# Six sums of four tokens on GpSimd instead of VectorE, and a new order of the instruction stream, in a fused attention and MoE kernel

## The chip, the cores and the metric

The kernel runs on one core of one Trainium2 chip. The metric is the device time of one launch in microseconds (us), as the median of several runs. The kernel before takes 362.11 us (three runs, 361.36 to 363.36).

The core has five instruction streams that run side by side [...]: TensorE (PE in the profile; PEld is its weight load), VectorE (DVE), ScalarE (ACT), GpSimd (POOL) and SyncE (SP, used here for DMA issues alone). Each executes its own stream in order.

## The reference, cut to what matters

```python
# q, k, v: (8, 8, 576, 64): batch, heads, tokens, head dimension; all float32
def _attn_ref(q, k, v):
    factor, scale = 4, 1.0 / np.sqrt(64)
    q_d, k_d, v_d = (x.reshape(B, H, S // 4, 4, D).mean(axis=3) for x in (q, k, v))
    out_d = softmax_attention(q_d, k_d, v_d)            # 144 x 144 scores
    out_up = np.repeat(out_d, 4, axis=2)
    mask = np.abs(pos[:, None] - pos[None, :]) < 4      # a band around the diagonal
    out_local = softmax_attention(q, k, v, where=mask)  # 576 x 576 scores, banded
    return out_up + out_local

def _moe_ref(x, w_in, w_out):                           # x: (4608, 512): tokens, heads * head dim
    h = x @ w_in                                        # d_ff = 2048
    g = np.where(h > 0, h, np.exp(np.minimum(h, 0)) - 1)
    return g @ w_out
```

So each token of each head attends to the seven tokens around it, and each group of four tokens attends, through its mean, to all groups. The two outputs are added, and the result goes through two dense products with an ELU between them.

## The kernel before

The kernel is written as a list of short words. One string, `ORDER`, holds all of them, and the kernel calls the function behind each word in turn. A word appends its instructions to the streams of its engines, so the order of the words is the order of the instructions on each engine; no scheduler changes it later.

```python
NINES, PE_SPREAD, HP4 = (0, 1, 2), (0, 1, 2), 12
X_DVE, K_DVE = ((0, 3, 0),), ((0, 0), (0, 1))
F_POOL = ()
ORDER = """
KM Lq0.0 KS KE Lk0.0 FILL TBL Lq0.1 KV Lk0.1 Lq0.2 KN Lk0.2 KI Cq0.0 KX Ck0.0 Lq0.3 Tq0.0 Lk0.3
... [cut]
"""
...
    ctx.enter_context(tc.manual_schedule())
    banks_as(("t", 4, 512))                       # batch 0: four single PSUM banks
    for word in ORDER.split():
        if word == "Q0":
            banks_as(("misc", 2, 512), ("hp", 2, 512))
        ...
        does[name](*numbers_of_the_word)
```

The numbers of a word are batch and pair of heads (there are eight batches of four pairs), or tile numbers of the MoE part. The words that matter here:

- `Lq Lk Lv`: load q, k or v of a pair through SyncE's queue. `Dq Dk b.h`: load two pairs of q or k through GpSimd's queue, converting to fp16. `WI WO`: load a quarter of w_in or w_out through GpSimd's queue.
- `Cq Ck Cv`: cast a loaded tile to fp16, on GpSimd.
- `Tq Tk`: transpose q or k with TensorE into PSUM. `Aq Ak`: copy them to SBUF (ScalarE; the k of pairs 0.0 and 0.1 by VectorE).
- `Fq Fk`: sums of four neighbouring tokens of the transposed q or k, for batches 0, 1 and 2 (`NINES`). Later batches get these sums out of TensorE together with the transposition.
- `SC` (batch 0: `SL` and `SD`): local scores, then scores of the groups. The latter read what `F` wrote.
- `E0 E1` (batch 0: `G H`): exponentials, ScalarE. `M`: the band mask, VectorE.
- `VS VD`: sums of four of v, TensorE, and their copy, VectorE. `OUT`: both attention outputs, TensorE. `DEN RC`: softmax denominators and their reciprocals. `RB`: reciprocals spread over partitions by TensorE. `LG MUL X`: outputs to SBUF, scaled, and added into the MoE input tile `xt`.
- `mm1.t.c` and `Q`: first MoE product, token tile t, d_ff tile c, four matmuls of 512 columns. `e m g`: exponential on ScalarE, then two VectorE instructions that make the ELU. `mm2.t.i`: a quarter of the second product of a 128-token tile. `oc st`: eviction by ScalarE and store.
- `Z1` to `Z3`: one to three filler matmuls, which compute nothing that is used. They go into the PSUM tile that the next word opens.
- `WL`: a one-element GpSimd write to a buffer; the next v load into that buffer waits for it. This word holds loads of v back.

The parts that the change touches or that its steps lead through:

```python
def load_half(n, b, h):                           # Dq, Dk
    t = sb.tile([128, 2, LR * D], FP16, tag=n + "2", bufs=2, name=n + "2")
    nc.gpsimd.dma_start(out=t[:], in_=...)        # fp32 in HBM, fp16 in SBUF

def hold(*_):                                     # WL
    t = stage("held")
    nc.gpsimd.memset(t[0:1, 0:1], 0.0)
    held.append(t)

def cast_v(b, j):                                 # Cv
    t = sb.tile([KW, NB, 2, D], FP16, tag="v16", bufs=7, name="v16")
    nc.gpsimd.tensor_copy(out=t[:], in_=...)

def fours(n, b, j):                               # Fq, Fk
    if n == "q":
        qt = stT[(b, j)][0]
        to, x = qt[:, S:RW], qt[:, 0:S]
    else:
        kt, kd = stT[(b, j)][-2:]
        to, x = kd[:], kt[:, PAD : PAD + S]
    x = x.rearrange("p (n h) -> p n h", h=4)      # 128 partitions, 144 groups of 4
    if (n, b, j) in F_POOL:
        f = sb.tile([128, SD], FP32, tag="four", bufs=1, name="four")
        nc.gpsimd.tensor_tensor(out=f[:], in0=x[:, :, 0], in1=x[:, :, 1], op=AB.add)
        nc.gpsimd.tensor_tensor(out=f[:], in0=f[:], in1=x[:, :, 2], op=AB.add)
        nc.gpsimd.tensor_tensor(out=to, in0=f[:], in1=x[:, :, 3], op=AB.add)
        return
    nc.vector.tensor_reduce(out=to, in_=x, axis=mybir.AxisListType.X, op=AB.add)

def elu_min(t, fc):                               # m
    nc.vector.tensor_scalar(out=e[:], in0=e[:], scalar1=1.0, scalar2=-1.0,
                            op0=AB.min, op1=AB.add)

def elu_add(t, fc):                               # g: reads the PSUM tile hp, and so frees it
    nc.vector.scalar_tensor_tensor(out=gts[t][:, fc, :], in0=hps[(t, fc)][:], scalar=0.0,
                                   op0=AB.max, in1=els.pop((t, fc))[:], op1=AB.add)
```

Of the kernel before, what the change touches and what calls it, by code (L numbers as in the profile page):

```python
# [51 lines left out]
g.0.1 Ak1.0 WLv2.0 Dq2.0 e.0.4 Fq1.1 Tk1.1 e.0.3 X0.2.1 mm1.0.7 Fk1.0 X0.3.1 Dk2.0 Ak1.1 m.0.3
g.0.3 SC1.0 m.0.4 mm1.0.9 E01.0 Fk1.1 m.0.2 E11.0 g.0.2 g.0.4 SC1.1 e.0.7 Cv1.0 Lv1.3 mm1.0.10
e.0.9 m.0.7 E01.1 g.0.7 mm1.0.6 M1.0 e.0.10 mm1.0.5 E11.1 m.0.9 m.0.10 VS1.0 g.0.9 e.0.6 Tq1.3
VD1.0 e.0.5 mm1.0.11 m.0.6 g.0.6 Dq2.1 Aq1.3 OUT1.0 m.0.5 M1.1 Tq1.2 LG1.0 g.0.10 Aq1.2 Tk1.3
Fq1.3 mm1.0.12 e.0.11 Dk2.1 Fq1.2 Ak1.3 Tk1.2 m.0.11 e.0.12 mm1.0.8 Fk1.3 Ak1.2 m.0.12 g.0.12
SC1.3 Cv1.1 Lv2.0 Fk1.2 E01.3 mm1.0.13 g.0.11 E11.3 VS1.1 g.0.5 VD1.1 e.0.8 mm2.0.0 M1.3 e.0.13
m.0.8 SC1.2 g.0.8 mm2.0.1 E01.2 m.0.13 g.0.13 mm1.0.15 E11.2 OUT1.1 e.0.15 M1.2 mm1.0.14 LG1.1
m.0.15 g.0.15 Z2 DEN1 e.0.14 m.0.14 g.0.14 Z1 mm2.0.2 RC1 Cv1.2 Lv2.1 Z1 RB1.0 Z2 VS1.2 MUL1.0
mm2.0.3 VD1.2 X1.0.1 RB1.1 oc.0.0 X1.0.2 OUT1.2 MUL1.1 st.0.0 mm2.0.4 LG1.2 X1.1.2 RB1.2 X1.1.1  # L60
Tq2.0 MUL1.2 mm2.0.5 Aq2.0 X1.2.1 Fq2.0 Tq2.1 Tk2.1 Aq2.1 mm2.0.6 X1.2.2 Ak2.1 Fq2.1 mm2.0.7
Fk2.1 Tq2.3 oc.0.1 Tk2.0 Aq2.3 mm2.0.8 Cv1.3 Lv2.2 st.0.1 Ak2.0 Fq2.3 mm2.0.9 Fk2.0 VS1.3 Tk2.3
VD1.3 Cv2.0 Lv2.3 mm2.0.10 Ak2.3 Fk2.3 OUT1.3 RB1.3 LG1.3 mm2.0.11 Cv2.1 Lq3.0 MUL1.3 VS2.0
oc.0.2 mm2.0.12 VD2.0 X1.3.1 st.0.2 SC2.0 Lk3.0 X1.3.2 mm2.0.13 E02.0 Cv2.2 mm1.1.0 E12.0
mm1.1.6 e.1.0 M2.0 Lv3.0 SC2.3 m.1.0 e.1.6 g.1.0 Cv2.3 mm2.0.14 E02.3 m.1.6 g.1.6 mm1.1.5 E12.3
Cq3.0 Lq3.1 Tq2.2 e.1.5 M2.3 mm1.1.3 Aq2.2 m.1.5 g.1.5 VS2.3 e.1.3 Ck3.0 Lk3.1 OUT2.0 Fq2.2
mm1.1.1 LG2.0 VD2.3 m.1.3 g.1.3 Tk2.2 e.1.1 VS2.1 Cv3.0 Lv3.1 Ak2.2 mm1.1.2 VD2.1 m.1.1 g.1.1
SC2.1 e.1.2 Cq3.1 Lq3.2 mm2.0.15 Fk2.2 E02.1 m.1.2 mm1.1.8 g.1.2 E12.1 Ck3.1 Lk3.2 mm1.1.4
oc.0.3 e.1.8 M2.1 st.0.3 SC2.2 e.1.4 m.1.8 mm2.1.0 g.1.8 E02.2 Cv3.1 Lv3.2 mm1.1.15 E12.2 m.1.4
g.1.4 OUT2.1 e.1.15 Lq3.3 M2.2 mm1.1.7 LG2.1 m.1.15 g.1.15 DEN2 e.1.7 Lk3.3 m.1.7 mm1.1.9 g.1.7  # L70
RC2 VS2.2 e.1.9 mm1.1.10 VD2.2 m.1.9 g.1.9 Cv3.2 Lv3.3 OUT2.2 e.1.10 RB2.2 LG2.2 m.1.10 mm1.1.14
g.1.10 Lq4.0 MUL2.2 OUT2.3 e.1.14 mm1.1.11 LG2.3 m.1.14 g.1.14 X2.2.2 RB2.3 Lk4.0 e.1.11 RB2.1
X2.2.3 MUL2.3 mm1.1.13 MUL2.1 X2.3.2 Tq3.1 e.1.13 Lv4.0 mm2.1.1 m.1.11 Aq3.1 g.1.11 X2.1.2 RB2.0
VD3.1 Cv3.3 mm1.1.12 Lq4.1 MUL2.0 X2.3.3 Tk3.1 e.1.12 m.1.13 mm2.1.2 g.1.13 X2.0.3 Ak3.1 X2.0.2
Tq3.0 KD3.1 m.1.12 Tk3.0 Aq3.0 g.1.12 Cq3.3 mm1.2.0 Ak3.0 VD3.0 Ck3.2 mm1.2.4 e.2.0 KD3.0 Ck3.3
Tq3.3 e.2.4 m.2.0 mm2.1.3 Aq3.3 g.2.0 Cq3.2 Tk3.3 m.2.4 oc.1.0 Lk4.1 mm1.2.11 g.2.4 X2.1.3 Ak3.3
Lv4.1 Cq4.1 VD3.3 mm2.1.4 st.1.0 e.2.11 KD3.3 Cv4.0 Lq4.2 SC3.3 m.2.11 mm1.2.7 g.2.11 E03.3
mm1.2.2 E13.3 mm2.1.5 e.2.7 M3.3 Lk4.2 e.2.2 SC3.1 m.2.7 g.2.7 mm2.1.6 E03.1 m.2.2 g.2.2 Cv4.1
Lv4.2 mm1.2.10 E13.1 Tq3.2 e.2.10 M3.1 Tk3.2 Aq3.2 m.2.10 mm1.2.3 g.2.10 Ck4.1 Lq4.3 Ak3.2 VD3.2
mm2.1.7 Ck4.0 e.2.3 KD3.2 SC3.2 m.2.3 oc.1.1 g.2.3 Cq4.0 mm2.1.8 E03.2 st.1.1 Lk4.3 mm1.2.13  # L80
E13.2 Cv4.2 Lv4.3 mm1.2.14 e.2.13 M3.2 SC3.0 e.2.14 m.2.13 mm2.1.9 E03.0 Lq5.0 g.2.13 m.2.14
mm2.1.10 E13.0 g.2.14 Tq4.1 M3.0 Tk4.1 Lk5.0 Aq4.1 Cq4.3 mm1.2.8 Ak4.1 Ck4.2 VD4.1 DEN3 e.2.8
KD4.1 m.2.8 Lv5.0 Tq4.0 g.2.8 Tk4.0 RC3 Aq4.0 Cq4.2 mm1.2.6 Ak4.0 Lq5.1 Ck4.3 VD4.0 mm1.2.5
e.2.6 KD4.0 SO3 SC4.1 m.2.6 e.2.5 g.2.6 mm2.1.11 Lk5.1 E04.1 m.2.5 g.2.5 mm1.2.15 E14.1 mm1.2.12
oc.1.2 M4.1 Lv5.1 e.2.15 st.1.2 SC4.0 e.2.12 m.2.15 mm2.1.12 g.2.15 E04.0 Lq5.2 m.2.12 mm1.2.9
E14.0 g.2.12 mm1.2.1 SI3 M4.0 Lk5.2 Tq4.2 e.2.9 Tk4.2 mm2.1.13 e.2.1 Ck5.1 Aq4.2 Lv5.2 mm2.1.14
m.2.1 Ak4.2 g.2.1 mm2.1.15 VD4.2 KD4.2 m.2.9 mm2.2.0 oc.1.3 g.2.9 st.1.3 mm2.2.1 SC4.2 mm2.2.2
E04.2 mm2.2.3 E14.2 OUT3.2 oc.2.0 M4.2 OUT3.3 st.2.0 MUL3.2 mm2.2.4 MUL3.3 mm2.2.5 X3.2.4 X3.2.3
OUT3.1 X3.3.4 OUT3.0 MUL3.1 mm2.2.6 X3.3.3 MUL3.0 Cv4.3 mm2.2.7 X3.1.3 Lq5.3 mm2.2.8 oc.2.1
X3.0.4 st.2.1 mm2.2.9 X3.0.3 X3.1.4 Tq4.3 Cv5.0 Tk4.3 Aq4.3 mm1.3.0 Cq5.1 Ak4.3 VD4.3 mm1.3.5  # L90
Cq5.0 e.3.0 KD4.3 SC4.3 m.3.0 e.3.5 Lk5.3 g.3.0 Ck5.0 mm2.2.10 E04.3 m.3.5 Lv5.3 mm1.3.9 g.3.5
Cv5.1 E14.3 Lq6.0 Cv5.2 Tq5.0 e.3.9 mm1.3.1 M4.3 Aq5.0 m.3.9 Tk5.0 e.3.1 VD5.0 DEN4 g.3.9 Ak5.0
Lk6.0 m.3.1 Tq5.1 g.3.1 mm1.3.13 KD5.0 Aq5.1 Cq5.3 RC4 Lv6.0 mm1.3.6 Cq5.2 VD5.1 SO4 e.3.13
Tk5.1 e.3.6 m.3.13 Tq5.2 g.3.13 Ck5.3 Ak5.1 Lq6.1 mm2.2.11 Aq5.2 m.3.6 KD5.1 Ck5.2 mm1.3.2 g.3.6
oc.2.2 VD5.2 Lk6.1 Tk5.2 e.3.2 mm1.3.10 st.2.2 Ak5.2 m.3.2 g.3.2 mm2.2.12 SI4 KD5.2 Lv6.1
mm1.3.4 e.3.10 SC5.0 e.3.4 m.3.10 mm2.2.13 g.3.10 Lq6.2 E05.0 m.3.4 mm1.3.11 E15.0 g.3.4 mm1.3.3
e.3.11 M5.0 SC5.2 m.3.11 e.3.3 g.3.11 Lk6.2 mm2.2.14 E05.2 m.3.3 g.3.3 mm1.3.14 E15.2 mm1.3.8
e.3.14 M5.2 mm2.2.15 m.3.14 e.3.8 g.3.14 OUT4.0 m.3.8 oc.2.3 g.3.8 OUT4.1 Cv5.3 Lv6.2 mm1.3.7
MUL4.0 st.2.3 Cv6.0 mm1.3.15 MUL4.1 e.3.7 X4.0.4 Lq6.3 OUT4.3 m.3.7 e.3.15 g.3.7 X4.1.5 OUT4.2
# [739 lines left out]
```

## Time and profile before

The profile is of one execution. Its span is 361.6 us, and the granted TensorE clock is 0.999.

| | |
|---|---|
| median time | 362.11 us |
| span of the profiled execution | 361.6 us |
| `F` on VectorE (TENSOR_REDUCE, 128 x 576 in, 128 x 144 out) | 24 of 744 to 745 ns |
| `m` (TENSOR_SCALAR) and `g` (SCALAR_TENSOR_TENSOR) | 144 each, mean 350 and 691 ns |
| `mm1` matmuls, `mm2` matmuls | 576 each, mean 379 and 380 ns |
| GpSimd cast of v | 30, mean 847 ns |
| load of v, issue to landing | 28 of 336 KB, median 7.0 us |
| data moved | 45.78 MB, mean 127 GB/s |

How to read it. [...] 379 ns isn't the pace at which 512-column matmuls follow each other: eight in a row take 1.73 us in the chain of waits late in the kernel, 0.216 us each. A group's idle time is that of its engine just ahead of it, with what ended it behind an arrow; an engine that isn't the bound may idle at no cost. A DMA share over 1.00 in a stretch means that packets of several queues were under way on an engine at once.

### The profile page before, as it was taken

The numbers are of one execution on the slowest core, as the hardware profiler recorded it, in microseconds if no ns is written. First come the engines' busy times: TensorE is split into PE (matmuls) and PEld (weight loads), VectorE is DVE, ScalarE is ACT, GpSimd is POOL, SyncE is SP. The second block draws the span as 40 slices with busy tenths as digits, with TensorE's granted clock in tenths as the row PEclk, the third lists the DMA queues.
The fourth block names the chain that finished last, engine by engine and source line by source line (L and its number), as shares of the span: only waits on it lengthen the run. The fifth ranks groups of instructions, "written<-read, shape, count | busy, mean of one in ns | idle before, by whom it ended". The sixth has DMA issues, their size and how long they took to land.

```text
span 361.6 us, 9574 instructions
## 1 busy us (share of the span) xinstructions
PE 350.0 (97%) x3964; PEld 183.4 (51%) x3964; DVE 240.1 (66%) x475; ACT 209.6 (58%) x395; POOL 121.2 (34%) x177
## 2 busy tenths in 40 slices
PE   7999899999999999999999999999999999999995
PEld 3664445554565545565555545554544544444442
DVE  3877996568887774587986675867665845465520
ACT  3855883578568875277587754685554334344421
POOL 6597314372293310860592109401500410000000
PEclk9999999999999999999999999999999999999999
DMA  7989999999968899498909992531004010010012
GB/s 265 176 140 198 197 197 203 201 177 166 189 120 168 152 200 198 128 188 168 205 4 198 170 156 83 83 84 62 29 32 113 30 60 29 29 61 29 30 60 87
DMA packets 106870, 45.78 MB, mean 127 GB/s; under 512 B 92330, under 2 KB 101194, under 8 KB 106826
## 3 DMA queue, kind: packets, MB, share of 16 engines
q1 hardware_dynamic: 96586, 34.61, 49.4%
q0 software_dynamic: 6528, 6.63, 10.9%
q10 hardware_dynamic: 3712, 3.93, 5.5%
q8 instruction: 31, 0.51, 0.6%
q14 instruction: 13, 0.11, 0.1%
HBM read 42.18 MB, written 9.53 MB: 143 GB/s over the span
## 4 chain that ended last, share of the span: by engine, by line
PE 73%; DMA 15%; DVE 5%; POOL 2%; ACT 2%; SPq 1%; issue 1%; ACTq 0%; POOLq 0%; DVEq 0%
PE op L754 31%; PE hp L710 27%; DMA v<-in_v_dram 11%; DMA rcb<-rd 3%; PE sc L528 2%; DVE e L739 2%; PE lg L653 2%; PE tq L409 2%; PE tq L433 2%; DVE gt L744 2%; DMA k<-in_k_dram 2%; PE tk L433 1%; PE den L602 1%; POOL WI L287 1%; ACT e L735 1%
## 5 line engine op out<-in xcount | busy, mean ns | idle before, releaser
L710 PE MATMUL hp<-xt,WI 128*128 128x512 f16 x576 | 140.7, 379 | 2.3 <-DVE gt L744 1.6
L754 PE MATMUL op<-WO,gt 128*128 128x512 f16 x576 | 138.8, 380 | 0.0
L735 ACT ACTIVATE e<-hp 128x512 f16<-128x512 f32 x144 | 85.7, 600 | 69.4 <-PE hp L710 66.5
L744 DVE SCALAR_TENSOR_TENSOR gt<-hp,e 128x512 f16<-128x512 f32 x144 | 99.3, 691 | 4.8
L739 DVE TENSOR_SCALAR e<-e 128x512 f16<-128x512 f16 x144 | 50.3, 350 | 54.9 <-ACT e L735 53.6
L710 PEld LDWEIGHTS <-WI 128*128 128x128 f16 x576 | 53.7, 97 | 64.0 <-issue 4.2
L754 PEld LDWEIGHTS <-gt 128*128 128x128 f16 x576 | 52.8, 98 | 59.3
L702 POOL TENSOR_TENSOR xt<-ln,gn 128x64 f16<-128x64 f16 (+7 forms) x63 | 41.2, 679 | 79.2 <-DVE ln L689 78.3
L559 ACT ACTIVATE pex<-sc 112x576 f16<-112x576 f32 x64 | 41.1, 648 | 9.8 <-PE sc L543 7.3
L761 ACT COPY os<-op 128x512 f32<-128x512 f32 x36 | 21.1, 587 | 41.6 <-PE op L754 35.8
L399 POOL CAST v<-v 112x768 f16<-112x768 f32 x30 | 25.1, 847 | 33.4 <-DMA v<-in_v_dram 18.4
L578 DVE TENSOR_TENSOR mex<-pex,MASK 112x1152 f16<-112x1152 f16 x32 | 25.3, 792 | 13.6 <-ACT pex L559 13.4
L394 POOL CAST k<-k 96x768 f16<-96x768 f32 x20 | 16.5, 834 | 28.8 <-PE tk L433 25.7
L565 ACT ACTIVATE dex<-sc 72x288 f16<-72x288 f32 x56 | 22.6, 404 | 0.0
L458 ACT CAST qt<-tq 128x720 f16<-128x720 f32 x20 | 15.2, 760 | 12.1 <-PE tq L409 11.3
L394 POOL CAST q<-q 96x768 f16<-96x768 f32 x20 | 17.2, 862 | 13.6 <-issue 6.6
L528 PEld LDWEIGHTS <-kt 64*112 64x112 f16 x384 | 12.4, 127 | 13.2 <-issue 7.6
L528 PE MATMUL sc<-qt,kt 64*112 64x96 f16 x384 | 16.7, 218 | 0.4 <-DVE kt L453 0.2
L409 PEld LDWEIGHTS <-VR 112*72 112x72 f16 x192 | 13.2, 113 | 4.6 <-issue 2.2
L689 DVE TENSOR_TENSOR ln<-lg,rcb 128x576 f16<-128x576 f32 x20 | 14.9, 746 | 0.0
L653 PEld LDWEIGHTS <-v 112*64 112x64 f16 x384 | 10.3, 109 | 8.5 <-issue 5.3
L653 PE MATMUL lg<-mex,v 112*64 112x96 f16 x384 | 13.7, 209 | 0.5 <-DVE ln L689 0.5
(72 smaller groups left out, 278.1 us busy)
## 6 DMA issues: line engine op xcount, KB each, us to landing
v<-in_v_dram SPq DMA_DIRECT2D x28, 336.0 KB, 7.0
out_dram<-os SPq DMA_DIRECT2D x36, 256.0 KB, 2.2
q<-in_q_dram SPq DMA_DIRECT2D x24, 288.0 KB, 6.5
k<-in_k_dram SPq DMA_DIRECT2D x24, 288.0 KB, 6.2
rcb<-rd ACTq DMA_DIRECT2D x10, 360.0 KB, 6.2
WI<-in_moe_w_in_dram POOLq DMA_DIRECT2D x4, 512.0 KB, 9.5
WO<-in_moe_w_out_dram POOLq DMA_DIRECT2D x4, 512.0 KB, 18.7
k<-in_k_dram POOLq DMA_DIRECT2D x4, 288.0 KB, 13.7
```

The costliest lines, as they stand in the source:

```text
L394: nc.gpsimd.tensor_copy(out=t, in_=x.rearrange("p (e c d) -> p c e d", e=2, d=D))
L399: nc.gpsimd.tensor_copy(out=t[:], in_=st32.pop(("v", b, j)).rearrange("p (e c) d -> p c e d", e=2))
L528: nc.tensor.matmul(sc[e][0:KW, c // 3, QB * (c % 3) : QB * (c % 3) + QB], kt[r, QB * c : QB * c + KW], q_of(b, j, r, c), start=True, stop= ...
L559: nc.scalar.activation(out=stS[(b, j)][2][:, e, :].rearrange("p (g u) -> p g u", g=2), in_=scs[(b, j)][e][0:KW, :, 0:HB], func=AF.Exp, sca ...
L578: nc.vector.tensor_tensor(out=mex[:], in0=pex[:], in1=mk2, op=AB.mult)
L653: nc.tensor.matmul(lg[64 * e : 64 * e + 64, c // 3, QB * (c % 3) : QB * (c % 3) + QB], v16[:, c, e, :], mex[:, e, QB * c : QB * c + QB], s ...
L702: eng.tensor_tensor(out=xts[t][:, j, t0 - TBLK * t : t1 - TBLK * t], in0=ln[:, a:z], in1=_rep4(gn[:, a // 4 : z // 4]), op=AB.add,)
L710: nc.tensor.matmul(hps[(t, fc)][:], WI[:, dc, 128 * fc : 128 * fc + 128], xts[t][:, dc, :], start=(dc == 0), stop=(dc == DMC - 1),)
L735: nc.scalar.activation(out=e[:], in_=hps[(t, fc)][:], func=AF.Exp)
L739: nc.vector.tensor_scalar(out=e[:], in0=e[:], scalar1=1.0, scalar2=-1.0, op0=AB.min, op1=AB.add)
L744: nc.vector.scalar_tensor_tensor(out=gts[t][:, fc, :], in0=hps[(t, fc)][:], scalar=0.0, op0=AB.max, in1=els.pop((t, fc))[:], op1=AB.add,)
L754: nc.tensor.matmul(ops[(t, tt)][:], gts[t][:, fc, 128 * tt : 128 * tt + 128], WO[:, fc, :], start=(fc == 0), stop=(fc == FCN - 1),)
```

## The change: sums to GpSimd, and a new order

The change has two parts. First, `F_POOL` names six of batch 1's eight sums of four tokens: k of all four pairs, and q of pairs 2 and 3. Those go by three GpSimd additions each, through an fp32 tile, instead of one VectorE reduction. The sums of q of pairs 0 and 1, and those of batches 0 and 2, stay on VectorE. The purpose is to take work from VectorE where it is busiest and to give it to an engine with room.

Second, `ORDER` is a new order of the same words. Both orders have the same 1534 words, each as often, among them the same fillers. Batch 0 has four single PSUM banks in both, and both have fillers beside batch 1's outputs. The functions are the same; the two settings are the whole change. The beginning of the diff, with cuts marked (the rest of it reorders words of batches 2 to 7 and of the MoE part in the same manner):

```diff
 RB_MORE = ()
-F_POOL = ()
+F_POOL = (('k', 1, 0), ('k', 1, 1), ('k', 1, 2), ('k', 1, 3), ('q', 1, 2), ('q', 1, 3))
 ORDER = """
... [cut: batch 0]
-OUT0.2 MUL0.1 WI2 LG0.2 OUT0.3 WI3 LG0.3 Z1 RB0.2 X0.0.1 WLv1.0 X0.1.1 Lv1.0 X0.1.0 MUL0.2 Z2
-RB0.3 Lv1.1 Lv1.2 Q0 MUL0.3 X0.2.0 Q1 X0.3.0 Dq1.1 Q2 Dk1.1 mm1.0.0 WO0 Tq1.0 e.0.0 mm1.0.1
-Aq1.0 WO1 Tk1.0 m.0.0 mm1.0.2 g.0.0 e.0.1 Tq1.1 WO2 e.0.2 Fq1.0 mm1.0.3 mm1.0.4 Aq1.1 WO3 m.0.1
-g.0.1 Ak1.0 WLv2.0 Dq2.0 e.0.4 Fq1.1 Tk1.1 e.0.3 X0.2.1 mm1.0.7 Fk1.0 X0.3.1 Dk2.0 Ak1.1 m.0.3
-g.0.3 SC1.0 m.0.4 mm1.0.9 E01.0 Fk1.1 m.0.2 E11.0 g.0.2 g.0.4 SC1.1 e.0.7 Cv1.0 Lv1.3 mm1.0.10
-e.0.9 m.0.7 E01.1 g.0.7 mm1.0.6 M1.0 e.0.10 mm1.0.5 E11.1 m.0.9 m.0.10 VS1.0 g.0.9 e.0.6 Tq1.3
... [cut]
-m.0.15 g.0.15 Z2 DEN1 e.0.14 m.0.14 g.0.14 Z1 mm2.0.2 RC1 Cv1.2 Lv2.1 Z1 RB1.0 Z2 VS1.2 MUL1.0
-mm2.0.3 VD1.2 X1.0.1 RB1.1 oc.0.0 X1.0.2 OUT1.2 MUL1.1 st.0.0 mm2.0.4 LG1.2 X1.1.2 RB1.2 X1.1.1
... [cut: same place in the new order]
+OUT0.2 MUL0.1 WI2 LG0.2 OUT0.3 WI3 LG0.3 Z1 RB0.2 WLv1.0 X0.0.1 Lv1.0 X0.1.0 MUL0.2 Lv1.1 Z2
+RB0.3 Lv1.2 X0.1.1 Q0 MUL0.3 X0.2.1 X0.2.0 Q1 X0.3.0 Dq1.1 Tq1.0 Q2 X0.3.1 Aq1.0 Dk1.1 Fq1.0
+mm1.0.0 WO0 mm1.0.3 e.0.0 mm1.0.2 Tk1.0 WO1 e.0.3 mm1.0.1 m.0.0 Tq1.1 g.0.0 e.0.2 WO2 Ak1.0
+m.0.3 mm1.0.4 g.0.3 WO3 e.0.1 m.0.2 Aq1.1 Tk1.1 m.0.1 e.0.4 g.0.1 Fk1.0 Ak1.1 g.0.2 mm1.0.7
+Dk2.0 m.0.4 g.0.4 SC1.0 e.0.7 Dq2.1 Fq1.1 mm1.0.9 E01.0 WLv2.0 Fk1.1 mm1.0.10 E11.0 Lv1.3 m.0.7
+mm1.0.6 e.0.9 g.0.7 Cv1.0 e.0.10 SC1.1 M1.0 e.0.6 mm1.0.11 E01.1 m.0.10 g.0.10 E11.1 m.0.9 VS1.0
... [cut]
+mm1.0.14 E11.2 Z1 mm2.0.2 e.0.14 M1.2 m.0.14 Z2 DEN1 g.0.14 Cv1.2 Lv2.1 Z2 VS1.2 RC1 Z1 RB1.0
+VD1.2 mm2.0.3 MUL1.0 OUT1.2 oc.0.0 X1.0.2 RB1.2 X1.0.1 LG1.2 st.0.0 mm2.0.4 MUL1.2 RB1.1 mm2.0.5
... [cut: the rest]
```

## The prediction, made before the changed kernel ran

> **What bounds the kernel now.** I read the page first (busy shares), then the chain of waits that ended last, then a table of stretches cut where the chain changes its nature, then each engine's timeline between 27 and 59 us, where the changed sums lie.
>
> The page's first part gives busy time, share and instructions of each engine:
>
> ```profile
> PE 350.0 (97%) x3964; PEld 183.4 (51%) x3964; DVE 240.1 (66%) x475; ACT 209.6 (58%) x395; POOL 121.2 (34%) x177
> ```
>
> TensorE is busy 350.0 of 361.6 us, so all idle together is 11.6 us. 1.47 us of that is the start, and 3.67 us of the last stretch (344.00 to 361.60, 13.93 busy) is the last eviction and store. That leaves about 6.5 us which any reordering could win, 1.8% of the time. No order of the same matmuls can be 2% faster unless hidden waits inside "busy" go as well.
>
> In the chain, the piece that stands out is a load of v:
>
> ```profile
> 28.64 28.66 DMA v<-in_v_dram
> 57.30 0.05 issue
> 57.35 0.84 POOL v L399
> 58.19 0.04 issue
> 58.23 0.49 PE vs L409 x6
> 58.73 0.86 PE op L754 x4
> ```
>
> This is the third v tile of batch 1 (word Lv1.2). It is issued at 28.64, lands at 57.30, is cast by GpSimd, and then VS1.2 starts on TensorE at 58.23. From there on the chain is nearly all TensorE. The stretches say the same (columns: length, then busy time and instructions of PE, PEld, DVE, ACT, POOL, granted clock, DMA share, GB/s):
>
> ```profile
> 27.00:58.20 31.20, 28.24 (x443) 14.72 (x440) 26.63 (x53) 21.37 (x44) 12.15 (x17) 1.00 1.21 197
> 58.20:100.00 41.80, 41.56 (x620) 22.50 (x620) 31.08 (x58) 27.24 (x55) 17.29 (x23) 1.00 1.10 186
> ```
>
> Before 58.2 TensorE idles 2.96 us, with DVE 85% busy and the DMA engines saturated; after it, up to 100 us, it idles 0.24 us. The idle pieces before the wall, in TensorE's timeline (start, length, what, and in brackets the idle time ahead and its releaser):
>
> ```profile
> 36.12 1.02 PE L710 MATMUL hp<-xt,WI 128*128 128x512 f16 x4 [0.57 <-DVE gt L744]
> 41.32 0.49 PE L409 MATMUL vs<-v,VR 112*72 112x128 f16 x6 [0.63 <-POOL v L399]
> 44.65 0.47 PE L426 MATMUL tk<-EYE,k 64*64 64x64 f16 x18 [0.57 <-ACT lg L677]
> 49.42 0.49 PE L409 MATMUL vs<-v,VR 112*72 112x128 f16 x6 [0.42 <-POOL v L399]
> ```
>
> Only the first is a wait for VectorE. Two of the others are waits for v tiles, as at 58.23 (0.31 us).
>
> [...] The trace agrees for tensor_scalar: alone it takes 0.29 us, and 0.84 us beside a GpSimd cast that ran from 91.79 for 0.83 us.
>
> ```profile
> 90.45 0.29 DVE L739 TENSOR_SCALAR e<-e 128x512 f16<-128x512 f16 x1
> 91.92 0.84 DVE L739 TENSOR_SCALAR e<-e 128x512 f16<-128x512 f16 x1 [0.45 <-ACT e L735]
> ```
>
> [...] the xt adds take 302 ns at 64 elements and 1079 at 512, so (1079-302)/448 = 1.73 ns per element and 191 ns fixed. [...] No add of this shape is in the trace. [...] the casts of v1.0, v1.1 and v1.2 start at 39.67, 48.54 and 57.35, 8.8 us apart, while GpSimd's queue pours in the weights. [...]
>
> **The change part by part.** The words of both orders are the same multiset, fillers included (27 by Z words in each), so TensorE, ScalarE and SyncE have the same work.
>
> *Sums.* Six reductions leave VectorE. They follow one another 0.66 us apart (0.745 each with the overlap at the ends), so VectorE is freed of 6 x 0.66 = 4.0 us. GpSimd gains 18 adds of 191 + 144 x 1.73 = 440 ns, 1.3 us per sum, say 1.4 with the waits between dependent adds, so 8 us. It has the room: 12.15 us busy in those 31.2. [...]
>
> *Where the sums stand in GpSimd's order.* GpSimd executes in order, and in the built program each of its DMA issues waits for the eighth GpSimd DMA before it. Before, two issues stood waiting for w_in's last two quarters:
>
> ```profile
> 34.55 0.70 POOL L357 DMA_DIRECT2D q<-in_q_dram  x1 [1.82 <-DMA WI<-in_moe_w_in_dram]
> 37.96 0.74 POOL L357 DMA_DIRECT2D k<-in_k_dram  x1 [2.14 <-DMA WI<-in_moe_w_in_dram]
> 39.67 1.59 POOL L399 CAST v<-held 112x768 f16<-112x768 f32 x1 [0.98 <-DMA held<-in_v_dram]
> ```
>
> After, the order is Fk1.0, Dk2.0, Dq2.1, Fk1.1, Cv1.0. Fk1.0 can run at 33.4 to 34.8, in time for its scores at about 35. But Dq2.1 inherits the wait to 37.96 and ends at 38.7, so Fk1.1 runs from 38.8 to 40.2. The down scores of pair 1 were done at 38.0 before; now TensorE must wait for 40.2. Two more tiles of the first MoE product stand ahead of them, so TensorE is there at about 38.6 and stands some 1.6 us. Then come one MoE tile (0.87) and VS1.0 at about 41.3, where it was. So the wait for VectorE at 36.12 turns into a wait for GpSimd, and the v tile decides again. The later sums (Fq1.3, Fk1.3, Fq1.2 after Dq2.0, which ended at 45.1) end near 46.5, 47.9 and 49.3, against scores at about 48; Fk1.2 follows Cv1.1 and an issue and ends near 52.2, for scores at about 52.7. These are close but fit.
>
> *The wall at v1.2.* Its landing follows from Lv1.0, which waits for a GpSimd word (WLv1.0) that now stands ahead of one 0.3 us add: 0.3 us earlier if the pace holds. TensorE should arrive in time, as it is ahead by one RB1.0 with its filler. But just these stand after the wall now: RB1.0 is 0.43 us and its filler 0.22, together 0.65 us of TensorE work that used to fill the wait. All sixteen tiles of the first product and parts 0 to 2 of the second stand before it in both.
>
> *Batch 0* keeps its bank layout and moves a few instructions by one or two places; I count zero. *Batches 2 to 7* are reordered with no work changed. One more q/k turn and one more reduction fall into the stretch after 74 us, where VectorE is over 85% busy; TensorE hardly idled there, so I count zero with a spread of 1 us either way.
>
> Sum: 362.1 - 0.3 + 0.65 = 362.45; I take 362.3, giving a little to whatever freed VectorE time does elsewhere.
>
> **The rivals.** (A) *The freed VectorE time reaches TensorE.* Then up to the 2.96 us of idle before 58.2 comes back: about 359.5. For it speaks VectorE's 85% and the wait at 36.12; against it, that most of the idle belongs to v tiles and bank hand-overs, and that the wall is a transfer. (B) *GpSimd's sums are slow or badly placed.* If an add takes 0.9 us [...], a sum is 2.7: Fq1.3, Fk1.3, Fq1.2 end at 47.8, 50.5, 53.2, the cast of v1.1 and Fk1.2 follow to 57, and exponent, mask and sums of pair 2 come after the wall: 4 to 5 us longer, 367. For it speaks the in-order queue; against it, the measured rate of the xt adds. (C) *The wall holds and the order after it decides*, my choice, within 1.5 us of before.
>
> **Range and chances.** C has about 70%, A 17%, B 13%. A's best reaches 359.5 and B's 367, neither of which is 2% (354.9 and 369.4). So: 362.3 us, 8 in 10 between 360.2 and 365.0; faster by over 2% 0.01, within 2% 0.96, slower by over 2% 0.03.
>
> **What would show it.** Right: the fours adds near 0.44 us each; VectorE's busy time lower by 3 to 4.5 us; the cast of v1.2 again starting at 57 to 57.4 after a wait for its load; SC1.1 with a wait of 1 to 2 us for GpSimd; TensorE's idle before 58 us still near 3 us. Wrong: VS1.2 not released by a load (the wall has moved), adds above 0.7 us, or a difference that arises after 60 us, which only the reordering of later batches could make.

## The result, and the profile after

The changed kernel takes 366.14 us (median of 4 runs, 365.58 to 366.54), the kernel before 362.56 us beside it (361.36 to 363.36). The ratio is 1.0101, with a 95% interval of 1.0067 to 1.0134: slower by about 3.6 us, where no change was predicted. It lies 1.1 us above the predicted range.

The first part of the page of the changed kernel (busy time and share of each engine):

```profile
PE 349.2 (96%) x3964; PEld 183.5 (50%) x3964; DVE 239.5 (66%) x469; ACT 210.1 (58%) x395; POOL 131.3 (36%) x195
```

The work of TensorE is the same, but its idle time rose from 11.6 to 15.6 us (span 364.8 less 349.2). VectorE has six reductions fewer and yet only 0.6 us less to do. The first says that the loss is made of waits; the second, that something on VectorE became dearer. All four runs have a mean clock of 0.999 or 1.000, so a lowered clock is no part of this loss. The stretches say where (changed kernel; length, then busy time and instructions of PE, PEld, DVE, ACT, POOL, granted clock, DMA share, GB/s):

```profile
27.00:58.20 31.20, 26.60 (x342) 13.24 (x341) 22.35 (x43) 21.16 (x44) 21.20 (x36) 1.00 1.21 198
58.20:100.00 41.80, 40.70 (x691) 22.69 (x693) 31.09 (x58) 25.72 (x52) 16.30 (x22) 1.00 1.03 177
100.00:180.00 80.00, 78.30 (x941) 43.49 (x936) 57.53 (x115) 55.06 (x104) 34.03 (x45) 1.00 0.96 165
```

TensorE's idle time, length less busy, stretch by stretch:

| stretch (us) | before | after | more |
|---|---|---|---|
| 0 to 27 | 3.19 | 3.61 | 0.42 |
| 27 to 58.2 | 2.96 | 4.60 | 1.64 |
| 58.2 to 100 | 0.24 | 1.10 | 0.86 |
| 100 to 180 | 0.64 | 1.70 | 1.06 |
| 180 to the end | 4.56 | 4.55 | -0.01 |

So there are two places: around the wall at 58 us, and after 100 us. (The 0.42 at the start scatters: with the same beginning of the order, the stretch has 2.55 us of idle time in e4's profile and 4.26 in e8's. It doesn't carry through: the GpSimd issue that waits for the fourth quarter of w_in starts at 37.77, before at 37.96.)

**First place.** TensorE's timeline (start, length, what, and in brackets the idle time ahead of it and its releaser):

```profile
40.77 0.32 PE L544 MATMUL sc<-qt,kd 64*72 64x144 f16 x4 [1.32 <-POOL kd L478]
...
50.41 0.32 PE L544 MATMUL sc<-qt,kd 64*72 64x144 f16 x4 [1.16 <-POOL kd L478]
...
52.83 0.49 PE L410 MATMUL vs<-v,VR 112*72 112x128 f16 x6 [1.14 <-POOL v L400]
...
59.20 0.44 PE L603 MATMUL den<-mex,IND 112*32 112x72 f16 x30 [0.86 <-DVE mex L579]
...
60.53 0.50 PE L410 MATMUL vs<-v,VR 112*72 112x128 f16 x6
```

The last line is VS1.2, the wall. It starts 2.30 us later than before (58.23) and **no longer waits for a load**: its v tile had landed and was cast by 58.5 (the last GpSimd line below). What came last was TensorE itself. Three of the four waits shown ahead of it are for GpSimd, whose timeline reads:

```profile
37.77 0.71 POOL L358 DMA_DIRECT2D q<-in_q_dram  x1 [1.36 <-DMA WI<-in_moe_w_in_dram]
...
39.05 1.10 POOL L477 TENSOR_TENSOR four<-four,kt 128x144 f32<-128x144 f32 x1
40.22 0.49 POOL L478 TENSOR_TENSOR kd<-four,kt 128x144 f16<-128x144 f32 x1
...
46.37 0.74 POOL L358 DMA_DIRECT2D q<-in_q_dram  x1 [4.82 <-PE tq L427]
47.12 0.44 POOL L476 TENSOR_TENSOR four<-qt 128x144 f32<-128x144 f16 x1
47.64 0.49 POOL L477 TENSOR_TENSOR four<-four,qt 128x144 f32<-128x144 f32 x1
48.21 0.49 POOL L478 TENSOR_TENSOR qt<-four,qt 128x144 f16<-128x144 f32 x1
...
51.94 0.83 POOL L400 CAST v<-v 112x768 f16<-112x768 f32 x1
...
57.71 0.82 POOL L400 CAST v<-v 112x768 f16<-112x768 f32 x1 [1.84 <-DMA v<-in_v_dram]
```

The line to read is the one at 46.37: the issue of Dq2.0 stood at the head of GpSimd's queue through 4.82 us of idling, until TensorE had read the old q tile in its buffer (word Tq1.2). Three sums then follow one another, 47.12 to 52.00, and the cast of v1.1 (51.94) comes behind them. In the kernel before, the issue that waited for Tq1.2 was Dq2.1, which had that buffer there. No sum stood between it and the cast, which waited for its load alone:

```profile
44.39 0.71 POOL L357 DMA_DIRECT2D q<-in_q_dram  x1 [3.12 <-PE tq L426]
48.54 0.82 POOL L399 CAST v<-v 112x768 f16<-112x768 f32 x1 [1.03 <-DMA v<-in_v_dram]
```

In the changed kernel the down scores of pair 3 wait for the second sum, VS1.1 for the cast, and the mask and denominators of pair 2 come so late that DEN1 waits once more.

**Second place.** TensorE's timeline again, all that it waited for between 100 and 195 us:

```profile
109.39 0.47 PE L434 MATMUL tq<-I,q 96*128 96x120 f16 x6 [1.64 <-DVE vd L506]
191.99 0.47 PE L434 MATMUL tq<-I,q 96*128 96x120 f16 x6 [0.72 <-DVE vd L506]
```

Both transpose a q of a later batch (Tq3.3, Tq6.2) into the PSUM tile that a v copy on VectorE has to free first. VectorE's timeline ahead of the first:

```profile
106.54 2.47 DVE L740 TENSOR_SCALAR e<-e 128x512 f16<-128x512 f16 x1
108.93 0.41 DVE L506 CAST vd<-tq 72x256 f16<-72x256 f32 x1
```

One `m` (m.1.13) takes 2.47 us instead of 0.28, with its input ready (its exponential ended at 105.56). GpSimd's timeline beside it:

```profile
104.90 0.85 POOL L703 TENSOR_TENSOR xt<-ln,gn 128x384 f16<-128x384 f16 x1 [0.92 <-DVE ln L690]
105.69 1.59 POOL L395 CAST q<-q 96x768 f16<-96x768 f32 x2
107.25 0.85 POOL L703 TENSOR_TENSOR xt<-ln,gn 128x384 f16<-128x384 f16 x1
108.04 0.82 POOL L400 CAST v<-v 112x768 f16<-112x768 f32 x1
```

From 104.90 to 108.86 five GpSimd instructions stand end to end (x2 is two casts), and `m` ends at 109.0, just after the last of them. The v copy, the next VectorE instruction, and so TensorE, come after that. The same group of `m` accounts for VectorE's missing relief: it sums to 54.8 us over the kernel, against 50.3 before. It is the order that does it: the order alone has 53.7 (e1), the sums alone 50.0 (e2). The group's line on the page of the changed kernel, and on that of the kernel before:

```profile
L740 DVE TENSOR_SCALAR e<-e 128x512 f16<-128x512 f16 x144 | 54.8, 382 | 56.4 <-ACT e L736 55.4
```

```profile
L739 DVE TENSOR_SCALAR e<-e 128x512 f16<-128x512 f16 x144 | 50.3, 350 | 54.9 <-ACT e L735 53.6
```

### The profile page after: what moved, and what is told of

It reads as the page before. It is cut to its first block, busy times and chain, and to the rows that moved or that the text cites. A ratio compares the mean times of both kernels' runs of the same rounds, so it can differ in the third digit from the quotient of the medians.

```text
span 364.8 us, 9591 instructions
## 1 busy us (share of the span) xinstructions
PE 349.2 (96%) x3964; PEld 183.5 (50%) x3964; DVE 239.5 (66%) x469; ACT 210.1 (58%) x395; POOL 131.3 (36%) x195
## 3 DMA queue, kind: packets, MB, share of 16 engines
q1 hardware_dynamic: 96586, 34.61, 49.3%
## 4 chain that ended last, share of the span: by engine, by line
PE 80%; DVE 5%; DMA 5%; POOL 3%; issue 3%; ACT 3%; SPq 0%; POOLq 0%; DVEq 0%; ACTq 0%
PE op L755 33%; PE hp L711 29%; DMA WI<-in_moe_w_in_dram 3%; PE sc L529 3%; PE lg L654 2%; DVE e L740 2%; PE den L603 2%; PE tq L410 2%; PE tq L434 2%; DMA q<-in_q_dram 2%; PE tk L434 1%; DVE gt L745 1%; PE vs L410 1%; PE lg L660 1%; PE sc L544 1%
## 5 line engine op out<-in xcount | busy, mean ns | idle before, releaser
L740 DVE TENSOR_SCALAR e<-e 128x512 f16<-128x512 f16 x144 | 54.8, 382 | 56.4 <-ACT e L736 55.4
L711 PEld LDWEIGHTS <-WI 128*128 128x128 f16 x576 | 53.7, 98 | 61.0 <-issue 1.4
L762 ACT COPY os<-op 128x512 f32<-128x512 f32 x36 | 21.1, 587 | 46.5 <-PE op L755 44.4
L395 POOL CAST q<-q 96x768 f16<-96x768 f32 x20 | 18.4, 930 | 12.5 <-issue 5.3
```

Of the source, the lines that this page charges most:

```text
L395: nc.gpsimd.tensor_copy(out=t, in_=x.rearrange("p (e c d) -> p c e d", e=2, d=D))
L711: nc.tensor.matmul(hps[(t, fc)][:], WI[:, dc, 128 * fc : 128 * fc + 128], xts[t][:, dc, :], start=(dc == 0), stop=(dc == DMC - 1),)
```

## The experiments

All of them are edits of `ORDER` and `F_POOL`. Where a word moves, the short diff shows its old and new neighbours. The ratio is to the kernel before on the same chip, with its 95% interval. Letters in the expectations: **Q** is the theory that GpSimd's queue (the sums, and a waiting issue ahead of the cast of v1.1) costs the time, **O** that the new order costs it by itself, and **L** that VectorE's `m` is held up while GpSimd runs end to end. Any other letter is explained where it stands. Line numbers of the source shift by up to five between kernels; the names tell which instruction it is.

| run | what | median (us) | ratio |
|---|---|---|---|
| changed | both parts | 366.14 | 1.0101 [1.0067, 1.0134] |
| e1 | new order alone | 364.58 | 1.0071 [1.0044, 1.0099] |
| e2 | sums alone | 369.65 | 1.0204 [1.0184, 1.0224] |
| e3 | changed, Dq2.0 later | 363.94 | 1.0048 [1.0032, 1.0064] |
| e4 | changed, three sums back | 365.00 | 1.0070 [1.0051, 1.0090] |
| e5 | e3, v copies ahead of two `m` | 362.85 | 1.0014 [0.9997, 1.0031] |
| e6 | new order after the wall alone | 364.04 | 1.0049 [1.0030, 1.0068] |
| e7 | before, the wall filled with work | see there | 1.0004 [0.9981, 1.0027] |
| e8 | e5, RB1.0 ahead of the wall | 363.17 | 1.0026 [1.0010, 1.0041] |
| e9 | e3, one GpSimd cast later | 362.93 | 0.9998 [0.9973, 1.0023] |
| e10 | e9, and more of the same | 361.80 | 0.9979 [0.9958, 1.0000] |

### e1 and e2: each part alone

```diff
# e1: ORDER is the new one, and
 F_POOL = ()
# e2: ORDER is the old one, and
-F_POOL = ()
+F_POOL = (('k', 1, 0), ('k', 1, 1), ('k', 1, 2), ('k', 1, 3), ('q', 1, 2), ('q', 1, 3))
```

> The new order with all sums on VectorE (F_POOL empty). Theory Q (GpSimd's queue: three sums of 1.65 us each and a DMA issue that waits for a transpose stand ahead of the cast of v1.1, which so starts at 51.94 instead of 48.54 us, and the mask, the denominators and VS1.2 follow late): the cast is back at 48 to 49.5, VS1.2 is released by its load at about 58.2, and what is left is RB1.0 and a filler behind it, 0.65 us: 362.6 to 363.7 us. Theory O (the new order itself costs, in batch 0's start or after 60 us, whoever does the sums): 365.3 to 366.5 us, with VS1.2 early and the loss elsewhere.

> The old order with the six sums on GpSimd. Theory Q: Fk1.0, Fk1.1 and the queue ahead of the cast of v1.1 delay SC1.0, SC1.3 and VS1.1 by 2 to 3 us each at their places; VS1.2 starts at 60 to 61 us instead of 58.2: 364.4 to 365.8 us. Theory O: the sums do no harm, VectorE is relieved of 4 us: 361.5 to 362.6 us.

*Measured, e1:* 364.58 us, between the two theories. With the sums on VectorE none of the waits for GpSimd's sums is there and the wall is a load again. In TensorE's timeline:

```profile
57.82 0.49 PE L408 MATMUL vs<-v,VR 112*72 112x128 f16 x6 [1.50 <-POOL v L398]
...
58.89 1.75 PE L753 MATMUL op<-WO,gt 128*128 128x512 f16 x4
```

VS1.2 is even earlier than before (57.82 against 58.23). The wait of 1.64 us at Tq3.3 and that of 0.73 at Tq6.2 are there too, so these belong to the order. The second line shows one more thing: four matmuls of 512 columns take 1.75 us, where they otherwise take 1.04. The granted clock of the stretch from 58.2 to 100 is 0.92 in this run. Over the runs of e1, those with a mean clock near 1.0 lie at 363.0 to 365.0, those at 0.991 to 0.995 at 364.9 to 367.2.

*Measured, e2:* 369.65 us, far above what either theory said, and VS1.2 starts at 65.16 instead of the 60 to 61 expected. The waits were of the expected kind, but one of them is long, and the clock fell in all four runs (mean 0.984 to 0.986):

```profile
52.94 0.46 PE L543 MATMUL sc<-qt,kd 64*72 64x144 f16 x4 [2.93 <-POOL kd L477]
53.33 1.89 PE L710 MATMUL hp<-xt,WI 128*128 128x512 f16 x4
```

The granted clock is 0.85 from 27 to 58.2 us in this profile, where it is 1.00 in the kernel before. The matmuls are slow twice there: after waits of 1.43 and 0.64 us, twelve of 512 columns take 3.77 us from 39.81, against 2.76 in the kernel before, and after the 2.93 us, two groups of four take 1.89 and 1.91 us, from 53.33 and from 55.64.

*What follows:* in the old order the sums are worse than in the new one, so the new order suits them better; the costs of the two parts don't add. And a wait may cost more than its length: here four 512-column matmuls take 1.75 us after a wait of 1.50 (e1) and 1.89 us after one of 2.93 (e2), instead of 1.04, in stretches with a granted clock of 0.92 and 0.85. That the wait is the cause is argued from the order of events alone.

### e3: only the waiting issue moved

```diff
-m.0.13 LG1.0 g.0.13 Dq2.0 Tk1.3 g.0.11 Tq1.2
+m.0.13 LG1.0 g.0.13 Tk1.3 g.0.11 Tq1.2
-E01.3 g.0.5 Cv1.1 m.0.15
+E01.3 g.0.5 Cv1.1 Dq2.0 m.0.15
```

> The changed kernel with one word moved: the GpSimd issue Dq2.0, which waited 4.8 us for the transpose of q1.2, stands behind the cast of v1.1 instead of ahead of the three sums. Theory Q: the sums start at 44.7 instead of 47.1, the cast of v1.1 at about 50 instead of 51.94, the waits for GpSimd at SC1.3 (1.16 us) and VS1.1 (1.14 us) nearly go, and VS1.2 starts at 58.5 to 59.2: 364.0 to 365.0 us. Theory O: 365.6 to 366.6 us, no change.

*Measured:* 363.94 us, with all six sums still on GpSimd. By the ratios, each taken on one chip, that is 1.9 us less than the changed kernel. TensorE's timeline, and two lines of GpSimd's:

```profile
50.21 0.49 PE L408 MATMUL vs<-v,VR 112*72 112x128 f16 x6 [0.35 <-POOL v L398]
...
57.70 0.49 PE L408 MATMUL vs<-v,VR 112*72 112x128 f16 x6 [0.16 <-POOL v L398]
```

```profile
44.33 0.42 POOL L474 TENSOR_TENSOR four<-qt 128x144 f32<-128x144 f16 x1 [3.33 <-ACT qt L452]
...
49.27 0.89 POOL L398 CAST v<-v 112x768 f16<-112x768 f32 x1
```

*What follows:* the down scores of pair 3 wait no more, VS1.1 starts 2.6 us earlier, and VS1.2 is back at its load, 2.8 us earlier than in the changed kernel (0.5 us of either is this profile's earlier start: SC1.1 runs at 40.28 instead of 40.77). The first sum still waits for its own input until 44.33, so the issue held the sums back by some 2.3 us, that earlier start allowed for, and not by all of the 4.82. The wait at SC1.1 (1.70 us) stays and costs nothing at the wall in this profile. This is the test of Q: it isn't the rate of the adds that costs the time, but their place behind an issue that waits. It takes both. In e1 the issue stands in the same place without sums behind it, and the cast of v1.1 still waits for its load (GpSimd's timeline in e1):

```profile
44.78 0.72 POOL L356 DMA_DIRECT2D q<-in_q_dram  x1 [4.28 <-PE tq L425]
48.13 0.82 POOL L398 CAST v<-v 112x768 f16<-112x768 f32 x1 [2.63 <-DMA v<-in_v_dram]
```

What is left, 0.5%, lies mostly after 100 us: the waits of 1.64 and 0.72 us for v copies are there as in the changed kernel.

### e4: three of the six sums back on VectorE

```diff
-F_POOL = (('k', 1, 0), ('k', 1, 1), ('k', 1, 2), ('k', 1, 3), ('q', 1, 2), ('q', 1, 3))
+F_POOL = (('k', 1, 0), ('k', 1, 1), ('k', 1, 2))
```

> The changed kernel with three of the six sums (q of pairs 2 and 3, k of pair 3) back on VectorE: GpSimd keeps k of pairs 0, 1 and 2. Theory Q: the cast of v1.1 starts at about 48.5 to 49, as soon as it has landed; SC1.3 doesn't wait for GpSimd; VS1.2 is released by its load at about 58.3; Fk1.1 still costs its wait of 1.3 us at SC1.1, but that lies ahead of the wall: 363.0 to 364.2 us. Theory O: 365.5 to 366.5 us.

*Measured:* 365.00 us, more than expected. The queue is relieved as expected (VS1.1 at 51.14 without a wait, VS1.2 at 58.33), but the wait at SC1.1 is now followed by slow matmuls, and the granted clock from 27 to 58.2 us is 0.95. TensorE's timeline:

```profile
40.10 0.32 PE L542 MATMUL sc<-qt,kd 64*72 64x144 f16 x4 [1.70 <-POOL kd L476]
...
42.12 1.91 PE L709 MATMUL hp<-xt,WI 128*128 128x512 f16 x4
```

*What follows:* the same wait of 1.70 us left the clock alone in e3's profile (1.00 from 27 to 58.2 us) and was followed by a lowered one in e4's (0.95), and in those of e5 and e9 below (0.95 each). Runs of e4 with a mean clock near 1.0 take 363.9 to 364.8 us, those at 0.993 to 0.994 some 365.2. So a wait of this length is a risk and not a certain loss: three of these four profiles have the lowered clock. As a test of Q alone e4 is blurred by it; its three runs near 1.0 lie where those of e3 do (362.8 to 364.7 us).

### e5 and e9: two ways to end the wait at Tq3.3

e5 moves the v copies ahead of two `m`; e9 leaves VectorE's and TensorE's words as they are in e3 and moves one GpSimd word, so that there is a gap between GpSimd's instructions.

```diff
# e5, on top of e3 (and the same for VD5.3, ahead of m.4.11)
-mm2.1.2 m.1.13 VD3.0 Cq3.2 g.1.13
+mm2.1.2 VD3.0 m.1.13 Cq3.2 g.1.13
# e9, on top of e3
-m.1.13 VD3.0 Cq3.2 g.1.13 Tk3.0 Tq3.3 X2.1.2 Ak3.0
+m.1.13 VD3.0 g.1.13 Tk3.0 Tq3.3 X2.1.2 Cq3.2 Ak3.0
```

> The changed kernel with Dq2.0 behind the cast of v1.1 (as in the run before), and two VectorE words moved: VD3.0 ahead of m.1.13 and VD5.3 ahead of m.4.11. Theory L (lock): m.1.13 took 2.47 us instead of 0.29 because GpSimd ran four instructions end to end, and TensorE waited 1.64 us at Tq3.3 for the copy behind it, and 0.72 us at Tq6.2 in the same manner. With the copies ahead, both waits of TensorE go, while m.1.13 itself still takes over 1.5 us: 1.5 to 2.4 us faster than with Dq2.0 moved alone (1.0048 of before), so 0.998 to 1.001 of before, 361.6 to 362.6 us. Theory W (the waits only move on, since TensorE has no other work there): 1.003 to 1.005 of before.

> The changed kernel with Dq2.0 behind the cast of v1.1, and one GpSimd word moved: Cq3.2 behind X2.1.2. No word of VectorE or TensorE is moved. Theory L (VectorE's tensor_scalar can't start while GpSimd runs instructions end to end, and gets in at the first gap): X2.1.2 must wait about 0.1 us for VectorE's ln, so a gap opens at the moment at which m.1.13 stands ready; m.1.13 takes 0.3 to 0.9 us instead of 2.46, TensorE's wait of 1.64 us at Tq3.3 goes, and the time is 1.3 to 1.8 us below that with Dq2.0 moved alone: 0.9995 to 1.0015 of before, 362.2 to 362.9 us. Theory E (m.1.13 waits for its exponential or for something else than GpSimd): m.1.13 stays above 2 us and the time stays at 1.004 to 1.006.

*Measured, e5:* 362.85 us, ratio 1.0014 against 1.0048 of e3, so some 1.2 us less, for 1.5 to 2.4 expected. Both waits for v copies are gone, but m.1.13 still takes 2.13 us, and the one who needs its ELU waits instead (VectorE's line, then TensorE's):

```profile
105.35 2.13 DVE L738 TENSOR_SCALAR e<-e 128x512 f16<-128x512 f16 x1
```

```profile
108.27 0.82 PE L753 MATMUL op<-WO,gt 128*128 128x512 f16 x3 [1.17 <-DVE gt L743]
```

*Measured, e9:* 362.93 us, ratio 0.9998, against 1.0048 of e3. VectorE's timeline, and GpSimd's beside it:

```profile
105.62 0.28 DVE L738 TENSOR_SCALAR e<-e 128x512 f16<-128x512 f16 x1
```

```profile
104.77 0.82 POOL L393 CAST q<-q 96x768 f16<-96x768 f32 x1
105.79 0.84 POOL L701 TENSOR_TENSOR xt<-ln,gn 128x384 f16<-128x384 f16 x1 [0.19 <-DVE ln L688]
```

*What follows:* with one cast less in the row, GpSimd idles 0.19 us, and `m` gets in just there, in 0.28 us. In that profile TensorE is busy 80.00 of the 80 us from 100 to 180, and the longest of all 144 `m` is 0.95 us instead of 2.47. The wait at Tq6.2 (0.73 us) is still there. No instruction was added, removed or moved on VectorE or TensorE, so it is the GpSimd instructions beside it that made m.1.13 long (2.46 us in e3, 0.28 here), though no wait for GpSimd is shown ahead of it. That much of L is shown. That `m` can't get in without a gap is not so. In the same trace a later `m` takes 0.46 us and ends at 110.34, just after the end of one GpSimd instruction (110.18), though the next one follows without a gap (VectorE's line, then GpSimd's):

```profile
109.88 0.46 DVE L738 TENSOR_SCALAR e<-e 128x512 f16<-128x512 f16 x1 [1.09 <-ACT e L734]
```

```profile
109.67 0.51 POOL L701 TENSOR_TENSOR xt<-ln,gn 128x192 f16<-128x192 f16 x1
110.13 0.89 POOL L393 CAST k<-k 96x768 f16<-96x768 f32 x1
```

In e5 too m.1.13 got in at 107.27 between two casts without a gap, and in the changed kernel no other of the 144 `m` takes over 0.91 us. That is no longer than one GpSimd cast of q (930 ns in the mean there). m.1.13 stood for longer and was passed over where one GpSimd instruction followed another (107.25 and 108.04 in the changed kernel); why just there stays open.

### e6: does the order after the wall cost by itself?

```diff
# the old order up to and with VS1.2, then the remaining words in the sequence of the new order
 ... Z1 RB1.0 Z2 VS1.2
-MUL1.0 mm2.0.3 VD1.2 X1.0.1 ...
+VD1.2 mm2.0.3 MUL1.0 OUT1.2 ...
 F_POOL = ()
```

> The old order, sums on VectorE, up to and with VS1.2; from there on the new order. If the new order after the wall costs by itself (theory L: waits of 1.64 and 0.72 us in place of 1.46 us in all): VS1.2 at 58.2 as before, the wait of 1.64 us at Tq3.3 again, 362.9 to 363.6 us, 1.002 to 1.004 of before. If all of the loss comes from ahead of the wall: 361.8 to 362.6 us, 0.999 to 1.001.

*Measured:* 364.04 us, ratio 1.0049, above the 1.002 to 1.004 expected. VS1.2 waits for the cast of its load, as in the kernel before. TensorE's timeline:

```profile
106.80 0.47 PE L432 MATMUL tq<-I,q 96*128 96x120 f16 x6 [1.63 <-DVE vd L504]
```

*What follows:* with no sum on GpSimd and an untouched wall, the order of batches 2 to 7 costs some 1.6 us (1.8 by the ratio). Its visible waits (1.63, 0.73 and 0.18 us, against 1.46 of all in the kernel before) account for about 1.1 us of it; the rest has no line of its own and stays open.

### e7 and e8: what stands ahead of the wall

```diff
# e7, on the kernel before
-RC1 Cv1.2 Lv2.1 Z1 RB1.0 Z2 VS1.2 MUL1.0 mm2.0.3
+RC1 Cv1.2 Lv2.1 Z1 RB1.0 mm2.0.3 VS1.2 MUL1.0
# e8, on top of e5
-Cv1.2 Lv2.1 Z2 VS1.2 RC1 Z1 RB1.0 VD1.2
+Cv1.2 Lv2.1 RC1 Z1 RB1.0 Z2 VS1.2 VD1.2
```

> The kernel before with one change at the wall: mm2.0.3 ahead of VS1.2, in place of its two fillers, which are left out. If the load of v1.2 is the wall, TensorE does 0.86 us of real work while it waits, in place of 0.43 us of fillers and 0.31 us of waiting: 0.5 to 0.8 us faster, 361.5 to 361.8 us. If the copy and the output behind VS1.2 are what counts, no change: 362.0 to 362.6 us.

> The run with the copies first, and RB1.0 with its filler ahead of VS1.2, as in the kernel before. If the 0.65 us of TensorE work behind the wall cost what the prediction said: 0.3 to 0.65 us faster than with the copies first alone, 361.0 to 362.0 us. If VS1.2 no longer waits for its load there, no change.

*Measured, e7:* ratio 1.0004, no change that its interval would show. Its mean clock was 0.986 to 0.995 in 11 of 22 runs, and the ratio leaves out the nine slowest of these; the median of the other 13 is 362.50 us. In its profile TensorE stands idle for 2.30 us at 158 us, far from the wall, with nothing shown that it waits for; the next eight 512-column matmuls take 3.03 us instead of 1.89, and the granted clock from 100 to 180 us is 0.98. Whether the edit brings this about isn't known, so e7 stays inconclusive. *Measured, e8:* 363.17 us, no better than e5 (362.85). RB1.0, moved ahead of the wall, meets a wait of its own there, 0.39 us for the reciprocal on VectorE.

*What follows:* moving 0.65 us of work from behind the wall to ahead of it gains nothing here. The reciprocal isn't ready so early, and in e5 the wall hardly waits any more.

### e10: what the experiments point to

```diff
# on top of e9
-m.4.11 g.4.11 Cq6.2 Ak5.3 mm1.4.2 oc.3.0 VD5.3
+VD5.3 m.4.11 g.4.11 Cq6.2 Ak5.3 mm1.4.2 oc.3.0
-Cv1.2 Lv2.1 Z2 VS1.2 RC1 Z1 RB1.0 VD1.2 mm2.0.3
+Cv1.2 Lv2.1 RC1 Z1 RB1.0 mm2.0.3 VS1.2 VD1.2
-F_POOL = (('k', 1, 0), ('k', 1, 1), ('k', 1, 2), ('k', 1, 3), ('q', 1, 2), ('q', 1, 3))
+F_POOL = (('k', 1, 0), ('k', 1, 2), ('k', 1, 3), ('q', 1, 2), ('q', 1, 3))
```

The sum of k of pair 1, the one behind the 1.3 to 1.7 us wait at SC1.1, goes back to VectorE, and two fillers at the wall give way to a piece of the second product.

> An attempt at a better version: the same with VD5.3 ahead of m.4.11, the sum of k of pair 1 back on VectorE (the sum for which TensorE waited 1.3 to 1.7 us at SC1.1), and at the wall RC1, RB1.0 and mm2.0.3 ahead of VS1.2 with its two fillers left out. Theories Q and L together: no wait for GpSimd at SC1.1, SC1.3 and VS1.1 over 0.5 us, none over 0.5 us at Tq3.3 and Tq6.2, VS1.2 at 57.7 to 58.3 with more work done ahead of it than before: 360.8 to 362.0 us, 0.995 to 0.9995 of before. If TensorE now idles long enough ahead of the wall that its clock is lowered, 363 us and more, with a granted clock of 0.99 to 0.995 in many runs.

*Measured:* 361.80 us (22 runs) beside 362.94 of the kernel before (35 runs). The wall in TensorE's timeline:

```profile
58.02 0.50 PE L408 MATMUL vs<-v,VR 112*72 112x128 f16 x6
```

*What follows:* the time is in the range expected. GpSimd idles 4.54 us before the load of v1.2 lands, so its queue has slack again, and VS1.2 starts at 58.02 without a wait, with mm2.0.3 already done. It beats the changed kernel by 1.2% (361.80 against 366.14, on different chips). Against the kernel before it is faster by 0.2%, with an interval that just reaches 1. So this change, mended and with two fillers fewer, is worth some 0.8 us, or between 0 and 1.5; which of the edits on top of e9 brings it wasn't separated.

## Why the prediction was wrong

Taken together, and by the ratios, the loss of 3.6 us splits into two nearly equal parts, each known to about 1 us. Moving one issue (e3) takes away 1.9 us; moving one cast as well (e9) takes away the rest.

1. *TensorE's idle time is all there is to win or lose.* Right: its busy time is 349.2, and the loss is idle time.
2. *The adds.* Right in rate: 0.43 to 0.50 us each, as 0.44 was worked out from the xt adds, save one of 0.63 us beside two `m` and two of 1.10 and 1.26 us beside a VectorE mask product. A whole sum is mis-sized: it takes 1.65 us from start to start (47.12, 48.78, 50.43), not 1.4, because each dependent add stands 0.07 us after the one before it and two of the three take 0.49.
3. *SC1.1 waits for Fk1.1.* Right in kind: 1.32 us in the changed kernel and 1.70 in e3, for 1.6 predicted. That it is so close is part luck: the sum ended at 40.71 for 40.2, and TensorE was there at 39.45 for 38.6, two errors of one sign. VS1.0 came at 42.11 instead of 41.3.
4. *"The later sums … after Dq2.0, which ended at 45.1 … end near 46.5, 47.9 and 49.3. … close but fit."* **The first step that failed.** They ended at 48.70, 50.35 and 52.00. The end at 45.1 was taken over from the profile of before (where the issue in that place is Dq2.1), but it is set by what the issue waits for. That is Tq1.2, which the new order puts later on TensorE (45.61 instead of 43.61), so the issue ended at 47.1. Two us from there and 0.7 from the sums' size put the third sum 2.7 us later than predicted, and the cast of v1.1 3.4 us later than before. e3 shows it: with only that issue moved, VS1.2 is back at its load.
5. *The wall holds (rival C).* Wrong: VS1.2 was not released by a load, the sign named for it. The load itself behaved nearly as predicted (cast at 57.71 after a wait for it, for 57 to 57.4). It was rival B that came, by its second cause alone: the sums are badly placed, not slow. B got 13%, argued down by the adds' rate, which says nothing of their place.
6. *Freed VectorE time reaches TensorE (rival A).* Rightly set aside. VectorE is busy 4.3 us less from 27 to 58.2, and TensorE there idles more. The sign named for it, 3 to 4.5 us less on VectorE over the kernel, failed at 0.6. It isn't the `m` beside the sums that took the relief: in that stretch the 15 `m` sum to 5.59 us, against 5.01 for 16, some 0.9 us more. It was lost to the `m` after 100 us (43.9 us against 39.4), which the new order made dearer.
7. *"Batches 2 to 7 … I count zero with a spread of 1 us."* **The second step that failed.** The order there costs some 1.6 us by itself (e6). Looking for work added to VectorE was the wrong question; what counted is which GpSimd words stand beside which `m`, and who stands behind that `m`. e9 shows it for the larger wait, the 1.64 us at Tq3.3.
8. *RB1.0 and its filler behind the wall, +0.65.* Not found (e8): once the wall waits no more than 0.2 us, there is no hole for them to fill.

## What to carry to other kernels

When an order changes, don't carry over the end of an instruction that waits: look up what it waits for, and move its time with that. In an in-order queue, put an issue that waits for a buffer behind all work that others are waiting for (worth 1.9 us in e3). Beside a run of GpSimd instructions without a gap, one `m` here took 2.47 us instead of 0.28, so look at what is behind such a VectorE instruction: one that frees a PSUM tile is better put ahead. Here another place for one word, or a gap of 0.2 us, was enough.

## What the runs showed of the hardware

- A VectorE tensor_scalar of 0.28 us alone stood for 2.47 us beside GpSimd instructions that followed one another without a gap, and took 0.28 us again where a gap of 0.19 us was made for it. This isn't the rule: other `m` got in between two GpSimd instructions without a gap (0.46 us in e9).
- Right after waits of 1.50 (e1), 1.70 (e4, e5, e9) and 2.93 us (e2), four 512-column matmuls took 1.75 to 1.91 us instead of 1.04; the granted clock of the stretch was 0.92 (e1), 0.95 (e4, e5, e9) and 0.85 (e2). After another wait of 1.70 us (e3), and after 1.64 us in the changed kernel, it was 1.00. What decides that wasn't found.
